# Hash-bucket attention before a relu-squared layer: attention in double steps of two key blocks, a shared ring of score banks, totals ahead of the last values

## The chip, the core and the metric

The kernel runs on one core of a Trainium2 chip. Engines with queues of their own work side by side: TensorE (PE, matmuls, with its weight loads, PEld, beside them), VectorE (DVE), ScalarE (ACT), GpSimd (POOL) and SyncE (SP, which here only issues DMAs). They meet in semaphores. Matmul results land in PSUM, which this kernel divides into 8 banks of 128 partitions x 512 float32. The metric is the device time of one execution in microseconds (us); the time of a kernel is the median of its runs.

## The reference

Attention in which a query sees only keys of its own hash bucket (six sign bits of a projection), and then a layer with squared relu. The bridge between the two lays the heads side by side.

```python
B, H, S, D = 4, 8, 768, 64
q_bits = (np.einsum('bhsd,dk->bhsk', q, proj) > 0)          # k_bits likewise
mask = q_bucket[:, :, :, None] == k_bucket[:, :, None, :]
scores = np.where(mask, scale * np.matmul(q, k.transpose(0, 1, 3, 2)), -1e9)
attn = np.exp(scores - scores.max(-1)); attn = attn / (attn.sum(-1) + 1e-09)
x = np.matmul(attn, v)                                      # -> (3072, 512)
r = np.maximum(x @ w_in, 0.0)                               # w_in 512 x 2048, float64 input
return (r * r) @ w_out                                      # w_out 2048 x 512, float64 input
```

## The kernel before

**Attention** goes over 16 pairs of heads (`pr`), each with six key blocks of 128 (`kt`). For a block, `score` computes the scores of all 768 queries against 128 keys for both heads of the pair: two cuts of the queries (512 and 256), each with two bf16 matmuls of hash bits, which push unequal buckets far down, and two float32 matmuls of features. Each cut has a PSUM tile of two banks, one bank a head (`st0`, `st1`, one buffer each), and ACT writes the exponential into `e`, a ring of four. `attend` multiplies `e` into the values, which accumulate in `xo` (two banks) over the six blocks. `add_up` keeps the running sum of the `e` tiles on DVE (`total`).

The end of a pair: `sum_up` adds over keys by matmuls with ones (`tot`), DVE transposes (`flip`), forms the reciprocal (`once`) and places it (`both`); `spread` carries it to the right partitions with one matmul into the last columns of `tot`'s bank, and DVE transposes that to `recs`; `normalize` multiplies `xo` by it into `x_t`, which SP stores to `x_all`.

The next pair is prepared meanwhile: `features` transposes q and k on DVE, `hash_bits` projects them on PE, `signs` makes bits of them on ACT, `weigh` scales the key bits on DVE. Two rotating banks (`bank`) serve `tot` and the hash.

The program order is that of the code; there is no scheduler. One step `u` is one key block: the score of block u, the spread if a pair ended, the hash of the next pair where the table `PREPARE` has it (block 3), the values of block u - 2, `sum_up` behind the values of block 4, and so on. Every engine takes its part of this order.

The **weights** come as float64 and are rounded to float32 in 32 pieces by integer operations on DVE (`part_weight`, `round_weight`) and ACT (`place_power`); the table `w_steps` spreads them over attention, two pieces a pair. `sums_in` and `sums_x` form sums of w_in and of x on DVE for the next stage, in the steps at the start of six pairs.

The **token stage** runs over three chunks of 1024 tokens. Both products are done by a scheme with seven products in place of eight, the second by it twice over (49 `leaf` tiles of w_out). In a chunk, `hidden(i, r)` for r = 0 to 7 multiplies x with `w_unit` r (SP loads it from the stored sums of w_in, two steps ahead): 28 matmuls of 512 columns, five results that ACT copies (`one`, `two`, `five`, `three`, `h`), and relu-squared on DVE. `project(i)` then multiplies with the leaves. During chunk 0, four sets of rows of w_out (`load_rows`) are turned into leaves: `sums_out(m)` forms first the smaller sums (`factors`), then `sums` in a single buffer, and POOL stores both to `w_out_49` in seven DMAs. That happens behind r = 0, 1, 3, 5 (`WHEN`). When the fourth is formed, its memory is given up for the buffers of the leaves, of which the first five are asked for at r = 6, on ACT's queue; such a transfer waits until the stores that read the old memory are done.

Lines that the prediction uses: L389 the score matmuls, L417 attend, L328 the hash, L435 the totals, L459 the spread, L394 the exponential, L644 all matmuls of the token stage, L651 ACT's copies there, L486 to L489 the sums, L545 `w_unit`, L773 the leaves.

Of the kernel before, what the change touches and what calls it, by code (L numbers as in the profile page):

```python
# [8 lines left out]
FP32 = mybir.dt.float32  # L9
# [25 lines left out]
def kernel(  # L35
# [257 lines left out]
    def first_features(w, r):  # L293

        if r == 0:
            feat[0, w] = p_f.tile([P, S], FP32, name=f"feat{w}")
        tp = bank("tp")
        for i in range(SB // 2):
            t = r * (SB // 2) + i
            nc.tensor.transpose(  # L300
                out=tp[:, i * P:(i + 1) * P],
                in_=nat[0, ("q_nat", "k_nat")[w]][:, t].rearrange("p h d -> p (h d)"),
                identity=ident,
            )
        out = feat[0, w][:, r * HS:(r + 1) * HS]
        if w == 0:
            nc.scalar.copy(out=out, in_=tp[:, 0:HS])
        else:
            nc.vector.tensor_copy(out=out, in_=tp[:, 0:HS])
# [8 lines left out]
    def hash_bits(pr, ws=(0, 1), banks=None):  # L318


        banks = banks or (bank("hash0"), bank("hash1"))
        for w in ws:
            hashed[pr, w] = banks
            for c in range(2):
                g = 2 * w + c
                for h in range(2):
                    rows = slice(h * D, (h + 1) * D)
                    nc.tensor.matmul(  # L328
                        out=banks[h][g * NR_B:(g + 1) * NR_B, 0:HS], lhsT=projs[rows],
# [3 lines left out]
    def signs(pr, w):  # L333
        bits[pr, w] = t = all_bits[pr % 2][w]
        for c in range(2):
            at = slice((2 * w + c) * NR_B, (2 * w + c + 1) * NR_B)
            for h in range(2):
                nc.scalar.activation(  # L338
                    out=t[h * D:h * D + NR_B, c * HS:(c + 1) * HS], in_=hashed[pr, w][h][at, 0:HS],
                    func=ACTF.Sign, scale=HUGE, bias=lifts[at],  # L340
                )

    def first_keys():

        bits[0, 1] = t = all_bits[0][1]
        for c in range(2):
            at = slice((2 + c) * NR_B, (3 + c) * NR_B)
            cut = slice(c * HS, (c + 1) * HS)
            for h in range(2):
                nc.vector.tensor_scalar(  # L350
                    out=t[h * D:h * D + NR_B, cut], in0=hashed[0, 1][h][at, 0:HS],
# [7 lines left out]
    def weigh(pr):  # L359
# [4 lines left out]

    PREPARE = (
        (),
        ((features, 0),),
        ((features, 1),),
        ((hash_bits,), (signs, 1)),
        ((signs, 0), (weigh,)),  # L370
        (),
    )

    weights = {}

    def score_banks(c):
        return ps_s.tile([P, 2, 512], FP32, name=f"st{c}")

    def score(pr, kt):
# [4 lines left out]
        sts = [score_banks(c) for c in range(2)]  # L384
        for st, (lo, hi) in zip(sts, CUTS):
# [7 lines left out]
        for st, (lo, hi) in zip(sts, CUTS):  # L393
# [780 lines left out]
```

## Time and profile before

| | us |
|---|---|
| runs shown | 936.61, 937.38, 939.73; median 937.38 |
| the profiled execution, device time | 935.12 |
| its span, first to last instruction | 933.4 |
| before the first score of pair 1 | 32.20 |
| pairs 1 to 14 | 307.88 |
| pair 15 and the end of attention | 26.49 |
| token stage | 566.83 |

| engine | busy us of 933.4 |
|---|---|
| PE | 902.5 |
| PEld | 492.8 |
| DVE | 697.8 |
| ACT | 363.4 |
| POOL | 91.4 |

The busy shares say that PE is the engine to look at. The mean clock granted to it was 0.995. PE's idle time has few places: the start, the end of attention, and some waits in chunk 0 of the token stage. In the timeline a row joins consecutive instructions of one kind: start, duration from the first start to the last end, operation, names, shape, count, and in brackets the idle time ahead of it with what ended it. A float32 matmul counts as two instructions there. Matmuls overlap at their ends, so the cost of one kind is read from the start of one row to the start of the next.

### The profile page before, as it was taken

Reading aid. Unit: us, or ns where it says so; the run is one execution under the profiler, and the core shown is the slowest. Engines: PE = TensorE matmul, PEld = TensorE weight load, DVE = VectorE, ACT = ScalarE, POOL = GpSimd, SP = SyncE. Lnnn points to the kernel's source line nnn. Section 1 sums busy time; section 2 is a strip of 40 time slices with the busy share of each in tenths; the row PEclk is TensorE's granted clock in tenths of the full one; section 3 lists DMA queues with packets and bytes.
Section 4 is the critical chain, followed back from the end, with each engine's and each line's share of the span. In section 5 each row is a group of like instructions: output and inputs, shape, how many; then the busy total and the mean of one; then the engine's idle time right before and its main releaser. Section 6 shows DMA issues by size and latency. Waiting matters only on the chain.

```text
span 933.4 us, 11806 instructions
## 1 busy us (share of the span) xinstructions
PE 902.5 (97%) x4326; PEld 492.8 (53%) x4326; DVE 697.8 (75%) x1010; ACT 363.4 (39%) x593; POOL 91.4 (10%) x149
## 2 busy tenths in 40 slices
PE   6999999999999999989799999999999999999995
PEld 2334343343334433434378884444888744448884
DVE  4777887788877776867876785667977856679775
ACT  4877777777767773212111112222111122221110
POOL 2000000000000000442300020111100211110002
PEclk9999999999999999999999999999999999999998
DMA  9665975799975422997885574556856634455565
GB/s 184 132 113 113 253 174 116 158 275 248 225 142 135 116 79 86 263 297 203 255 279 154 163 149 96 146 147 198 293 156 166 136 113 138 137 154 157 152 168 104
DMA packets 253343, 158.14 MB, mean 169 GB/s; under 512 B 166432, under 2 KB 215584, under 8 KB 253280
## 3 DMA queue, kind: packets, MB, share of 16 engines
q1 hardware_dynamic: 219264, 83.12, 38.6%
q10 hardware_dynamic: 23280, 38.81, 14.1%
q0 software_dynamic: 10736, 35.40, 12.5%
q8 instruction: 36, 0.59, 0.3%
q14 instruction: 27, 0.22, 0.1%
HBM read 119.28 MB, written 38.01 MB: 169 GB/s over the span
## 4 chain that ended last, share of the span: by engine, by line
PE 86%; DMA 6%; DVE 4%; issue 1%; ACT 1%; POOL 1%; SPq 0%; DVEq 0%; ACTq 0%
PE acc L644 50%; PE st L389 17%; PE xo L417 14%; DMA w_unit<-w_in 3%; PE tot L435 2%; PE hash L328 2%; DMA leaf<-w_out 1%; DMA w_out<-sums 1%; DMA out_dram<-ot 1%; PE tot L459 1%; DVE b L734 1%; POOL w_out L933 1%; ACT e L394 0%; DMA k_nat<-in_k_dram 0%; DVE h L733 0%
## 5 line engine op out<-in xcount | busy, mean ns | idle before, releaser
L394 ACT ACTIVATE e<-st 128x1024 f32<-128x1024 f32 x192 | 145.3, 810 | 87.4 <-PE st L389 87.0
L644 PE MATMUL acc<-x,w_unit 128*128 128x512 f32 x384 | 169.5, 593 | 0.6 <-DMA w_unit<-w_in 0.6
L389 PE MATMUL st<-feat,feat 64*128 64x512 f32 (+1 forms) x768 | 150.3, 483 | 0.0
L417 PE MATMUL xo<-e,v_nat 128*64 128x512 f32 (+1 forms) x768 | 144.9, 498 | 0.2 <-DVE x_t L472 0.2
L644 PE MATMUL acc<-t_x,w_unit 128*128 128x512 f32 x288 | 129.6, 600 | 7.2 <-ACT one L651 7.1
L644 PE MATMUL acc<-b,leaf 128*128 128x256 f32 x600 | 133.2, 379 | 0.2 <-DMA leaf<-w_out 0.2
L644 PEld LDWEIGHTS acc<-b,leaf 128*128 128x128 f32 x600 | 113.9, 190 | 17.4 <-issue 1.4
L644 PEld LDWEIGHTS acc<-x,w_unit 128*128 128x128 f32 x384 | 72.8, 190 | 91.5 <-issue 89.0
L644 PEld LDWEIGHTS acc<-t_x,w_unit 128*128 128x128 f32 x288 | 54.9, 192 | 78.6 <-issue 68.2
L417 PEld LDWEIGHTS xo<-e,v_nat 128*64 128x64 f32 x768 | 46.9, 136 | 86.5 <-issue 84.4
L407 DVE TENSOR_TENSOR total<-total,e 128x1536 f32<-128x1536 f32 x48 | 83.5, 1740 | 1.1 <-ACT e L394 1.0
L389 PEld LDWEIGHTS st<-feat,feat 64*128 64x128 f32 x768 | 66.5, 189 | 33.9 <-issue 31.5
L733 DVE TENSOR_TENSOR h<-acc,two 128x512 f32<-128x512 f32 x24 | 16.6, 691 | 86.6 <-PE acc L644 86.6
L644 PE MATMUL acc<-t,leaf 128*128 128x256 f32 x336 | 76.5, 380 | 0.3 <-DVE t L492 0.3
L651 ACT COPY two<-acc 128x512 f32<-128x512 f32 (+1 forms) x45 | 21.9, 486 | 132.7 <-PE acc L644 129.6
L338 ACT ACTIVATE bits<-hash,lifts 32x384 bf16<-32x384 f32 x120 | 68.6, 572 | 4.8 <-PE hash L328 3.3
L644 PEld LDWEIGHTS acc<-t,leaf 128*128 128x128 f32 x336 | 63.7, 190 | 9.7 <-DVE t L492 1.1
L651 ACT COPY one<-acc 128x512 f32<-128x512 f32 (+1 forms) x45 | 21.9, 486 | 120.1 <-PE acc L644 65.1
L389 PE MATMUL st<-bits,bits 64*128 64x256 bf16 (+1 forms) x384 | 63.6, 328 | 4.3 <-ACT e L394 2.5
L734 DVE SCALAR_TENSOR_TENSOR b<-h 128x512 f32<-128x512 f32 x96 | 64.3, 690 | 2.9 <-DMA x_all<-x_t 0.5
L644 PE MATMUL acc<-b_t,leaf 128*128 128x256 f32 x240 | 54.2, 380 | 1.3 <-issue 1.3
L389 PEld LDWEIGHTS <-bits 64*128 64x128 bf16 x384 | 18.9, 93 | 68.3 <-issue 67.9
(125 smaller groups left out, 898.8 us busy)
## 6 DMA issues: line engine op xcount, KB each, us to landing
leaf<-w_out ACTq DMA_DIRECT2D x147, 256.0 KB, 3.0
w_unit<-w_in SPq DMA_DIRECT2D x24, 896.0 KB, 5.4
raw<-in_moe_w_in_dram SPq DMA_DIRECT2D x16, 512.0 KB, 4.3
raw<-in_moe_w_out_dram SPq DMA_DIRECT2D x16, 512.0 KB, 3.9
w_out<-sums POOLq DMA_DIRECT2D x16, 448.0 KB, 8.2
v_nat<-in_v_dram SPq DMA_DIRECT2D x16, 384.0 KB, 4.3
x_all<-x_t SPq DMA_DIRECT2D x16, 384.0 KB, 3.0
x<-x_all POOLq DMA_DIRECT2D x3, 2048.0 KB, 12.0
```

What stands on the lines that cost most here:

```text
L328: nc.tensor.matmul(out=banks[h][g * NR_B:(g + 1) * NR_B, 0:HS], lhsT=projs[rows], rhs=feat[pr, w][rows, c * HS:(c + 1) * HS], start=True, ...
L338: nc.scalar.activation(out=t[h * D:h * D + NR_B, c * HS:(c + 1) * HS], in_=hashed[pr, w][h][at, 0:HS], func=ACTF.Sign, scale=HUGE, bias=li ...
L389: nc.tensor.matmul(out=st[:, h, 0:hi - lo], lhsT=src[pr, 1][rows, key], rhs=src[pr, 0][rows, lo:hi], start=first, stop=not first,)
L394: nc.scalar.activation(out=e[:, :, lo:hi], in_=st[:, :, 0:hi - lo], func=ACTF.Exp, scale=scale)
L407: nc.vector.tensor_tensor(out=totals[pr], in0=in0, in1=weights[pr, kt][:, :, 0:S], op=ALU.add)
L417: nc.tensor.matmul(out=xo[h * D:(h + 1) * D, lo:hi], lhsT=nat[pr, "v_nat"][:, h, kt * D:(kt + 1) * D], rhs=weights[pr, kt][:, h, lo:hi], s ...
L435: nc.tensor.matmul(out=tot[g * 32:(g + 1) * 32, 0:HS], lhsT=ones, rhs=src[:, h, c * HS:(c + 1) * HS], start=src is totals[pr], stop=src is ...
L459: nc.tensor.matmul(out=rec, lhsT=picks, rhs=both.rearrange("p c n -> p (c n)"), start=True, stop=True)
L644: nc.tensor.matmul(out=acc[to], lhsT=a(i), rhs=b(i), start=first and i == 0, stop=last and i == n - 1, skip_group_check=True,)
L651: nc.scalar.copy(out=t, in_=acc[of])
L733: nc.vector.tensor_tensor(out=h, in0=one, in1=two, op=ALU.add)
L734: nc.vector.scalar_tensor_tensor(out=out[:, r], in0=h, scalar=0.0, in1=h, op0=ALU.max, op1=ALU.mult)
```

## The change

Attention goes in double steps: two scores, then the values of two blocks. In pair `pr` the order on PE is: scores 0 and 1; `finish` of the pair before (the hash of the pair after, the totals, the values of blocks 4 and 5, the spread); scores 2 and 3; values 0 and 1; scores 4 and 5; values 2 and 3. The totals so stand ahead of the last two values. One pool of three double banks, taken in turn, serves the score tiles, the totals, the hash and the first transposes. The spread's result goes to the last 24 columns of `xo`, by two matmuls of 64 output partitions instead of one of 128, and the transpose to `recs` moves into `normalize`. Both feature tiles of the next pair are made ahead of a pair's first score, and the weight pieces, loads and sums are put at fixed places of a pair; sums follow at a pair's end.

At the start, all transposes come ahead of both hashes, and pair 1 is loaded before the first values. In the token stage the second set of `sums` is formed and stored behind r = 2 instead of 1 (`THEN`), its `factors` still behind r = 1; `load_unit` stands ahead of the leaves; and the first five leaves of chunk 0 are asked for on SP's queue.

```diff
-    ps_s = first.enter_context(tc.tile_pool(name="ps_s", bufs=1, space=PSUM))
+    ps_s = first.enter_context(tc.tile_pool(name="ps_s", bufs=3, space=PSUM))
-    ps_1 = first.enter_context(tc.tile_pool(name="ps_1", bufs=2, space=PSUM))
-    def bank(name):
-        return ps_1.tile([P, 512], FP32, name=name, tag="bank")
+    def turn(name):
+        return ps_s.tile([P, 2, 512], FP32, name=name, tag="turn")
...
     def spread(pr):
-        both, tot = onces.pop(pr)
-        rec = tot[:, HS:HS + 2 * NB]
-        nc.tensor.matmul(
-            out=rec, lhsT=picks, rhs=both.rearrange("p c n -> p (c n)"), start=True, stop=True
-        )
...
+        both = onces.pop(pr)
+        rec = outs[pr][:, 1024 - 2 * NB:]
+        for h in range(2):
+            nc.tensor.matmul(
+                out=rec[h * D:(h + 1) * D], lhsT=picks[:, h * D:(h + 1) * D],
+                rhs=both.rearrange("p c n -> p (c n)"), start=True, stop=True,
+            )
+        recs[pr] = rec
...
+    def finish(pr, beside=None):
+        tot = turn("tot")
+        if beside:
+            beside()
+        sum_up(pr, tot)
+        for kt in (SB - 2, SB - 1):
+            attend(pr, kt)
+        spread(pr)
...
+        first_features(0)
+        first_features(1)
         for w in range(2):
+            hash_bits(0, turn("hash"), (w,))
         signs(0, 0)
         first_keys()
+        for pr in range(NP):
+            a, b = 2 * pr, 2 * pr + 1
+            more = pr + 1 < NP
+            def prepare():
+                hash_bits(pr + 1, turn("hash"))
+                for w in (1, 0):
+                    signs(pr + 1, w)
...
+            if more and pr > 0:
+                for w in range(2):
+                    features(pr + 1, w)
+            if pr > 0:
+                round_weight(b - 2)
+                load_weight(b)
+            score(pr, 0)
+            score(pr, 1)
+            if pr > 0:
+                finish(pr - 1, prepare if more else None)
+            add_up(pr, 1)
...
+            if pr > 0:
+                normalize(pr - 1)
...
+            part_weight(a)
+            score(pr, 2)
+            score(pr, 3)
+            if pr == 0:
+                prepare()
+            place_power(a)
+            attend(pr, 0)
+            attend(pr, 1)
+            for kt in (2, 3):
+                add_up(pr, kt)
...
+            round_weight(a)
+            part_weight(b)
...
+            score(pr, 4)
+            score(pr, 5)
+            place_power(b)
+            attend(pr, 2)
+            attend(pr, 3)
+            add_up(pr, 4)
+            if pr in sums:
+                f, n = sums[pr]
+                f(n)
+        finish(NP - 1)
+        normalize(NP - 1)
+        round_weight(2 * NP - 1)
...
-        def load_leaf(n):
+        def load_leaf(n, early=False):
...
-                nc.scalar.dma_start(out=leaves[k, m], in_=w_out_49[OUTER[k][0], :, m])
+                queue = nc.sync if early else nc.scalar
+                queue.dma_start(out=leaves[k, m], in_=w_out_49[OUTER[k][0], :, m])
...
-        NOUT, WHEN = 2, (0, 1, 3, 5)
+        NOUT, WHEN, THEN = 2, (0, 1, 3, 5), (0, 2, 3, 5)
...
                 if i == 0 and r in WHEN:
-                    m = WHEN.index(r)
-                    sums_out(m)
+                    sums_out(WHEN.index(r))
+                if i == 0 and r in THEN:
+                    m = THEN.index(r)
+                    sums_out_49(m)
...
+                load_unit(i * NR + r + (3 if i == 0 and r < 2 else 2))
                 if r == NR - 2:
                     for n in range(NLEAF - 2):
-                        load_leaf(n)
-                load_unit(i * NR + r + (3 if i == 0 and r < 2 else 2))
+                        load_leaf(n, i == 0)
```

The first place is PE at the end of a pair. Before, the totals came behind the values of block 4 (`e_119`), with those of block 5 (`e_120`) still to come; these are the rows around `tot` in a middle pair.

```order
L417 MATMUL xo<-e_119,v_nat 64x512 x2
L417 MATMUL xo<-e_119,v_nat 64x257 x2
L435 MATMUL tot<-total,ones 32x384 x4
L435 MATMUL tot<-e_120,ones 32x384 x4
L389 LDWEIGHTS bits_0_122
```

In the changed program the same place reads so, again in a middle pair; the row ahead is the last of score 1.

```order
L375 MATMUL st<-feat_2105,feat_2107 128x256 x2
L327 MATMUL hash<-feat_2298,projs 32x384 x4
L327 MATMUL hash<-feat_2300,projs 32x384 x4
L420 MATMUL tot<-total,ones 32x384 x4
L420 MATMUL tot<-e_115,ones 32x384 x4
L402 MATMUL xo<-e_114,v_nat 64x512 x2
L402 MATMUL xo<-e_114,v_nat 64x257 x2
L402 MATMUL xo<-e_115,v_nat 64x512 x2
L402 MATMUL xo<-e_115,v_nat 64x257 x2
L445 MATMUL xo<-both,picks 64x24 x2
```

The hash moved here from behind score 3, and the totals, both last values and the spread now stand in one run, behind two scores of the next pair.

The second place is DVE behind `hidden(0, 1)` of the token stage, where the second set of factors and sums is formed. Before:

```order
L492 TENSOR_TENSOR b_t<-b_3246,b_3245 128x512
L486 TENSOR_TENSOR factors<-other,factors 128x512
L487 TENSOR_TENSOR factors<-factors,other 128x512
L488 TENSOR_TENSOR factors<-factors 128x512
L489 TENSOR_TENSOR factors<-factors 128x512
L486 TENSOR_TENSOR sums<-factors 128x896
L487 TENSOR_TENSOR sums<-factors 128x896
L488 TENSOR_TENSOR sums<-sums,factors 128x896
L489 TENSOR_TENSOR sums<-factors,sums 128x896
L492 TENSOR_TENSOR b_3246<-b_3248,b_3246 128x512
L733 TENSOR_TENSOR h<-acc_3396,one 128x512
```

And now:

```order
L481 TENSOR_TENSOR b_t<-b_3241,b_3240 128x512
L475 TENSOR_TENSOR factors<-other,factors 128x512
L476 TENSOR_TENSOR factors<-factors,other 128x512
L477 TENSOR_TENSOR factors<-factors 128x512
L478 TENSOR_TENSOR factors<-factors 128x512
L481 TENSOR_TENSOR b_3241<-b_3243,b_3241 128x512
L746 TENSOR_TENSOR h<-acc_3373,one 128x512
```

The four operations on `sums` left this place; they follow the next r-step.

The third place is the queue that asks for the first leaves. Before, it was ACT, between the copies of r = 6 and those of r = 7:

```order
L651 COPY three<-acc_3598 128x512
L731 COPY h<-acc_3598 128x512
L773 DMA leaf<-w_out_66 128x512 x5
L651 COPY one<-acc_3652 128x512
L651 COPY two<-acc_3652 128x512
```

Now it is SP, behind the units up to that of the next chunk's first step:

```order
L519 DMA w_unit<-w_in_63 128x14x128 x6
L787 DMA leaf<-w_out_66 128x512 x5
L519 DMA w_unit<-w_in_63 128x14x128
L818 DMA out_dram<-ot 32x16x32 x24
```

Nothing stands now between ACT's copies of r = 6 and r = 7, and the five leaves have one w_unit and then the output stores behind them on SP.

More of the change, by code (lines that the diff above doesn't have):

```diff
@@ L316, with hash_bits @@
     hashed = {}
-    def hash_bits(pr, ws=(0, 1), banks=None):
-        banks = banks or (bank("hash0"), bank("hash1"))
+    def hash_bits(pr, banks, ws=(0, 1)):
         for w in ws:
@@ L328, in hash_bits @@
                     nc.tensor.matmul(
-                        out=banks[h][g * NR_B:(g + 1) * NR_B, 0:HS], lhsT=projs[rows],
+                        out=banks[g * NR_B:(g + 1) * NR_B, h, 0:HS], lhsT=projs[rows],
                         rhs=feat[pr, w][rows, c * HS:(c + 1) * HS], start=True, stop=True,
@@ L425, with sum_up @@
     onces = {}
-    def sum_up(pr):
-        tot = bank("tot")
+    def sum_up(pr, tot):
+        tot = tot[:, 0]
         for src in (totals[pr], weights[pr, SB - 1]):
```

156 lines of the change are left out of this document (53 added, 103 removed).

## The prediction

> **What bounds the kernel now.** I read the stages first, since a share of the whole span mixes attention with the product that follows it. The rows below are busy time by stretch of time; after the stretch and its length come TensorE (PE), its weight loads, VectorE (DVE), ScalarE (ACT), GpSimd, the granted clock, the DMA share and GB/s. The cuts are the first score of the second head pair (32.20), that of the last pair (340.08) and the first matmul of the token stage (366.57).
>
> ```profile
> 32.20:340.08 307.88, 307.61 (x2156) 122.08 (x2157) 255.16 (x347) 228.55 (x339) 0.79 (x1) 1.00 0.73 171
> 340.08:366.57 26.49, 25.09 (x174) 10.23 (x173) 16.79 (x25) 12.04 (x17) 0.00 (x0) 1.00 0.11 41
> 366.57:933.40 566.83, 547.00 (x1852) 350.81 (x1851) 409.06 (x591) 103.63 (x210) 84.59 (x126) 0.99 0.63 176
> ```
>
> In the fourteen middle pairs PE is busy for 307.61 of 307.88 us, so nothing but less time on PE makes them shorter: 307.88 / 14 = **21.99 us a pair**. The last pair and the token stage hold idle time, 1.4 and 19.8 us.
>
> What PE spends a pair on is in its timeline (start, duration, operation). Durations overlap, since matmuls are pipelined, so I use start to start.
>
> ```profile
> 170.93 0.40 PE L459 MATMUL tot<-both,picks 128*128 128x24 f32 x2
> 171.26 1.51 PE L417 MATMUL xo<-e,v_nat 128*64 128x512 f32 x8
> 172.71 0.39 PE L389 MATMUL st<-bits,bits 64*128 64x512 bf16 x2
> 172.94 1.02 PE L389 MATMUL st<-feat,feat 64*128 64x512 f32 x4
> 173.80 0.27 PE L389 MATMUL st<-bits,bits 64*128 64x256 bf16 x2
> 173.91 0.60 PE L389 MATMUL st<-feat,feat 64*128 64x256 f32 x4
> 174.43 1.51 PE L417 MATMUL xo<-e,v_nat 128*64 128x512 f32 x8
> ...
> 177.60 1.23 PE L328 MATMUL hash<-feat,projs 64*32 64x384 f32 x16
> 178.77 1.51 PE L417 MATMUL xo<-e,v_nat 128*64 128x512 f32 x8
> ...
> 189.71 0.85 PE L435 MATMUL tot<-total,ones 128*32 128x384 f32 x8
> 190.38 0.83 PE L435 MATMUL tot<-e,ones 128*32 128x384 f32 x8
> 191.14 0.39 PE L389 MATMUL st<-bits,bits 64*128 64x512 bf16 x2
> ```
>
> A score (S) takes 174.43 - 172.71 = 1.72, an attend (A, weights times values) 172.71 - 171.26 = 1.45, the hash 1.17, the totals 1.43, the spread 0.33. Six S, six A and the three others make 19.02 + 2.93 = 21.95, which is the period. The same run shows what it costs to go from one kind to the other. The 512-column half of S takes 173.80 - 172.71 = 1.09; the 256-column half should take half of that, 0.545, and takes 0.63, so leaving S for A costs about 0.09 and S alone is 1.635. For A there is one place with three in a row:
>
> ```profile
> 359.40 4.10 PE L417 MATMUL xo<-e,v_nat 128*64 128x512 f32 x24
> 363.44 0.85 PE L435 MATMUL tot<-total,ones 128*32 128x384 f32 x8
> 364.11 0.83 PE L435 MATMUL tot<-e,ones 128*32 128x384 f32 x8
> 366.33 0.40 PE L459 MATMUL tot<-both,picks 128*128 128x24 f32 x2 [1.40 <-DVE both L449]
> ```
>
> Three take 4.04, so one more costs (4.04 - 1.45) / 2 = 1.30, and entering and leaving A cost 0.15. A visit to A between scores costs 0.15 + 0.09 = **0.24**.
>
> **The change, part by part.**
>
> *Double steps.* S and A now alternate two by two: three visits a pair instead of six. The new pair: three S S (2 x 1.635 + 0.09 = 3.36 each, 10.08); two A A between scores (2 x 1.30 + 0.15 = 2.75, 5.50); one A A behind the totals (2.65); totals 1.43; hash and spread below. Saved in S and A: 3 x 0.24 = 0.72.
>
> *Hash.* It took 1.17 because its second half waited for a transposed feature tile on DVE. In the first pair, where both tiles are there, it takes 23.00 - 22.19 = 0.81:
>
> ```profile
> 12.57 0.39 PE L389 MATMUL st<-bits,bits 64*128 64x512 bf16 x2 [1.81 <-DVE bits L354]
> ...
> 14.94 0.39 PE L389 MATMUL st<-bits,bits 64*128 64x512 bf16 x2 [0.57 <-ACT e L394]
> ...
> 22.19 0.88 PE L328 MATMUL hash<-feat,projs 64*32 64x384 f32 x16
> 23.00 1.51 PE L417 MATMUL xo<-e,v_nat 128*64 128x512 f32 x8
> ```
>
> The new program has DVE make both tiles ahead of the pair's first score, so I take 0.81, bounded by 0.81 and 1.17.
>
> *Spread.* Two matmuls of half the width stand behind A A, with A's shape, into A's own bank. No row shows this form. Bounds: 0.13 (the 24 columns added as a share of A's time per column, with one start) is below what the row of one 24-column matmul with both switches took, 0.33, and two of those would be 0.66. I take 0.25, nearest the one measured.
>
> Sum of a pair: 10.08 + 5.50 + 2.65 + 1.43 + 0.81 + 0.25 = **20.72**; 14 x (21.99 - 20.72) = **-17.8**.
>
> *Does anything stall in its place?* Three places decide. First, the ring of three score banks. The exponential of the 512-column half starts 1.30 after its S and takes 1.03 (S at 191.14 above):
>
> ```profile
> 192.44 1.03 ACT L394 ACTIVATE e<-st 128x1024 f32<-128x1024 f32 x1 [1.67 <-PE st L389]
> ```
>
> A double step takes four banks; the fourth is the first again, free 1.30 + 1.03 = 2.33 after the start, and wanted at 1.635 + 1.09 = 2.73: 0.4 to spare. The totals reuse the third bank, whose exponential starts no earlier than 1.635 + 1.30 = 2.94 and ends at 3.97; the totals are wanted at 3.36 + 0.81 = 4.17: 0.2 to spare. Were the cover gone, each late exponential would hold PE for what it is late, and behind it stand the last values and the spread. Second, the reciprocal: spread came 366.33 - 363.44 = 2.89 after the totals with DVE free, a row above; A A now lies between and takes 2.65 of it plus the 1.43 of the totals themselves, so it is covered. Third, DVE, whose work is the same but regrouped: in the pair with the most of it, where a quarter of the input sums is formed, it is busy 19.52 of 21.93 us.
>
> ```profile
> 169.21:191.14 21.93, 21.93 (x158) 8.71 (x155) 19.52 (x27) 16.25 (x24) 0.00 (x0) 1.00 0.67 181
> ```
>
> In a pair of 20.72 that leaves 1.2, less the places where DVE waits for ACT or PE; covered, but barely, in six pairs. ACT has 16.25 of work.
>
> *Start.* The first score waits 1.81 for the key bits. All transposes now come ahead of both hashes, and the first keys' features are copied without a hash between. I expect -1.2 there, and -0.2 from the first pair's fewer visits net of its own waits for exponentials (0.57 each now): **-1.4**, bounds 0 and -3 (all of 1.81, two times 0.57).
>
> *Last pair.* The 26.49 of the second row become one pair without hash (19.91) plus totals, A A and spread (1.43 + 2.65 + 0.25): 24.24, **-2.3**; the 1.40 wait for the reciprocal goes, since A A stands in it.
>
> *Token stage.* The second set of factor sums is formed and stored one r-step later, and the first five leaves of w_out go out on SP's queue, behind the w_unit of that step, instead of ACT's.
>
> ```profile
> PE acc L644 <- ACT one L651: 7.1, 2, 4.8
> ...
> PE acc L644 <- DMA w_unit<-w_in: 0.6, 1, 0.6
> ```
>
> ```profile
> 400.94 1.09 DVE L486 TENSOR_TENSOR sums<-factors 128x896 f32<-128x896 f32 x1 [4.65 <-DMA w_out<-sums]
> ```
>
> The waits of PE for one ACT copy are 2.3 and 4.8 us. The first stems from DVE, which stood 4.65 for the earlier sums to be stored; with the second sums an r-step later their buffer is free. The third set then follows after one r-step, 28 matmuls or some 12 us, with its own smaller sums ahead of it, where before the second followed in less because DVE was late with the first; I expect no wait there. The second stems from ACT's own queue:
>
> ```profile
> 455.83 6.05 ACTq L773 DMA_DIRECT2D leaf<-w_out  x5
> 461.98 0.58 ACT L651 COPY one<-acc 128x512 f32<-128x512 f32 x1 [5.97 <-DMA w_out<-sums]
> ```
>
> Five leaf transfers hold ACT for 6.05 us until those stores land, with the copy behind them. On SP's queue they hold only SP, and behind them there is just the next w_unit. After this gap PE ran at a granted clock of 0.53 for 3.6 us, which costs 3.6 x 0.47 = 1.7 more:
>
> ```profile
> 462.40:466.00 3.60, 3.38 (x4) 1.50 (x5) 1.38 (x2) 0.16 (x1) 0.00 (x0) 0.53 1.02 365
> ```
>
> The Trainium skill, "TensorE: Matmul & The Clock Gate", section "Why this matters for your kernels", warns of PE-idle gaps above about 3 us, after which the clock falls back; the trace agrees with 4.8 us and 0.53. By that rule a wait for leaves of 2.6 us would leave the clock alone and the sum as it stands, and one of 5 would bring the 1.7 back.
>
> So 2.3 + 0.6 + 4.8 + 1.7 = 9.4 can go. What is late next are the leaves, behind 0.9 MB of w_unit in the same queue.
>
> ```profile
> w_unit<-w_in SPq DMA_DIRECT2D x2, 896.0 KB, 16.4
> ```
>
> ```profile
> leaf<-w_out ACTq DMA_DIRECT2D x5, 256.0 KB, 8.9
> ```
>
> ```profile
> 472.93 1.24 PE L644 MATMUL acc<-b,leaf 128*128 128x256 f32 x5
> ```
>
> The leaf products would start at 472.93 - 9.4 = 463.5 (on the old clock of events). If leaves land as before, 8.9 after an issue at 455.83 - 2.9, they are there (461.8): no wait. If they follow w_unit, issued near 451.5 and landed 16.4 later, the first arrives at about 468: 4.5. I take 2.6, between them: **-6.8**, bounds 0 and -9.4.
>
> **Sum**: -17.8 - 1.4 - 2.3 - 6.8 = -28.3. The profiled execution (935.12 us, its span 933.4) would be at 906.8; the median of the runs lies 2.3 above it, 937.38, so I give **909.1** against that.
>
> **Rivals.**
>
> 1. *The token stage's waits only move* (24%). For it: 0.9 MB of w_unit takes 16.4 us beside the stores, and moved stores may meet another w_unit; against it: waits of an engine off the path have slack here, 19.8 us idle in 567. It gives attention's 21.5 alone: 937.4 - 21.5 = **915.9**.
> 2. *DVE becomes the bound in the full pairs* (12%). For it: 19.52 of a 20.72 pair, and the next pair's features stand behind the sums; a hash that waits for them holds totals and values behind it. At 1.5 us in six pairs it gives back 9: **918**. Against it: the other pairs show DVE idle, 255.16 of 307.88 busy.
> 3. *The change of kind costs nothing by itself* (8%): 0.24 would be a shadow of the shapes, so that double steps save only the hash, the spread, start and waits, 0.72 x 15 = 10.8 less: **920**. Against it: the three A in a row take 4.04 and not 4.35.
> 4. *Slower: scores back to back run into the exponential* (5%). At the start, where each S must wait for the last one's banks, S comes every 14.94 - 12.57 = 2.37 with 0.57 idle: 0.73 more than 1.635. If the second score of every double step paid that, 48 x 0.73 = 35 would be lost against 28.3 gained: **944**. It decides once PE waits above 28.3 / 48 = 0.59 per double step. Against it: the third bank, by which the fourth half is 0.4 late-proof; a margin of 0.2 at the totals is the weakest.
>
> **How the numbers follow.** My forecast, 909 within 4 us, has 51%. The range takes in rival 1 and most of 2 and reaches down to all 9.4 in the token stage and a cheap start: **902 to 918.5**, with rivals 3, 4 and their like outside. A difference of 0.3%, 2.8 us, is about what a measurement of this kernel can tell from no change. Forecast and rivals 1 to 3 are all faster by far more: faster 0.94, same 0.02 (several stalls at once), slower 0.04.
>
> **What would show it.** Right: in the middle pairs PE still has no idle time and first scores lie 20.7 apart; spread starts without a wait; PE's two waits for the ACT copy are gone and the clock stays at 1.00 there; the leaf products wait under 3 us. Wrong: waits of scores or totals for the exponential, of the hash for features in pairs with sums, of w_unit or leaf above 3 us, or a second A that takes 1.45.

## The result, and the profile after

The changed kernel takes **909.25 us** (median of 4 runs, 908.39 to 909.83) against 937.25 of the kernel before (4 runs, 936.61 to 939.73): ratio 0.970, 95% interval 0.968 to 0.972. The forecast was 909.1. That is closer than its parts were, as the stages show. They are cut at the same events as before: first score of pair 1, first score of pair 15, first matmul of the token stage. Columns are as in the prediction (length, busy time of PE, PEld, DVE, ACT, POOL, clock, DMA share, GB/s); this is the changed kernel.

```profile
35.17:322.92 287.75, 287.75 (x2188) 131.41 (x2187) 253.31 (x343) 227.77 (x336) 0.79 (x1) 1.00 0.76 176
322.92:346.90 23.98, 23.98 (x178) 10.97 (x176) 15.94 (x24) 11.56 (x16) 0.00 (x0) 1.00 0.18 61
346.90:906.50 559.60, 545.64 (x1854) 350.12 (x1850) 410.65 (x594) 104.01 (x210) 84.80 (x126) 1.00 0.64 179
0.00:35.17 35.17, 25.17 (x149) 11.85 (x150) 17.55 (x51) 20.81 (x31) 6.09 (x22) 1.00 1.04 171
```

| stage | before, us | after, us | change | forecast |
|---|---|---|---|---|
| to the first score of pair 1 | 32.20 | 35.17 | +3.0 | -1.4 |
| 14 middle pairs | 307.88 | 287.75 | -20.1 | -17.8 |
| last pair | 26.49 | 23.98 | -2.5 | -2.3 |
| token stage | 566.83 | 559.60 | -7.2 | -6.8 |
| span | 933.4 | 906.5 | -26.9 | -28.3 |

PE is busy in all 287.75 us of the middle pairs: no stall took the place of what was removed, and a pair takes 20.55. The start went the wrong way by 4.4 us against its forecast, and the pairs gave 2.3 more than theirs. That 28.3 forecast and 26.9 measured both end near 909 is also due to which run was profiled: that of the changed kernel, 908.39, lies 0.9 below its median, that of the kernel before, 935.12, lay 2.3 below the one it was held against.

PE in a middle pair of the changed kernel (start, duration, operation), from the hash to the second double step:

```profile
38.51 0.88 PE L327 MATMUL hash<-feat,projs 64*32 64x384 f32 x16
39.31 0.85 PE L420 MATMUL tot<-total,ones 128*32 128x384 f32 x8
39.98 0.83 PE L420 MATMUL tot<-e,ones 128*32 128x384 f32 x8
40.74 2.81 PE L402 MATMUL xo<-e,v_nat 128*64 128x512 f32 x16
43.38 0.26 PE L445 MATMUL xo<-both,picks 128*64 128x24 f32 x4
43.56 0.39 PE L375 MATMUL st<-bits,bits 64*128 64x512 bf16 x2
...
46.90 2.81 PE L402 MATMUL xo<-e,v_nat 128*64 128x512 f32 x16
49.64 0.39 PE L375 MATMUL st<-bits,bits 64*128 64x512 bf16 x2
```

From start to start: hash 0.80, totals 1.43, A A behind them 2.64, spread 0.18, S S 46.90 - 43.56 = 3.34, A A 2.74. Each is the term of the forecast (0.81, 1.43, 2.65, 0.25, 3.36, 2.75) or a little less, and no row has a wait in brackets.

What PE waits for in the token stage of the changed kernel is short now (total, times, longest, from the waits of PE):

```profile
PE acc L657 <- DMA leaf<-w_out: 2.3, 2, 2.1
...
PE acc L657 <- DMA w_unit<-w_in: 0.6, 1, 0.6
PE acc L657 <- ACT one L664: 0.5, 2, 0.3
```

The waits for ACT's copy of 2.3 and 4.8 are gone, and the leaves are late by 2.1, where the forecast had 2.6. The 0.6 for a w_unit stayed.

### The profile page after: what moved, and what is told of

Its sections match the earlier page's. It is cut to its first block, busy times and chain, and to the rows that moved or that the text cites. A ratio compares the mean times of both kernels' runs of the same rounds, so it can differ in the third digit from the quotient of the medians.

```text
span 906.5 us, 11859 instructions
## 1 busy us (share of the span) xinstructions
PE 882.5 (97%) x4358; PEld 504.4 (56%) x4358; DVE 697.4 (77%) x1010; ACT 364.2 (40%) x593; POOL 91.7 (10%) x149
## 4 chain that ended last, share of the span: by engine, by line
PE 90%; DMA 4%; DVE 2%; ACT 1%; issue 1%; POOL 0%; ACTq 0%; SPq 0%; DVEq 0%
PE acc L657 54%; PE st L375 18%; PE xo L402 14%; DMA w_unit<-w_in 3%; PE tot L420 3%; PE hash L327 1%; ACT bits L337 1%; DMA out_dram<-ot 1%; DVE peaks L698 0%; DMA q_nat<-in_q_dram 0%; PE tp L300 0%; POOL out_dram L818 0%; DVE b L747 0%; ACTq L787 0%; DVE ot L811 0%
## 5 line engine op out<-in xcount | busy, mean ns | idle before, releaser
L375 PE MATMUL st<-feat,feat 64*128 64x512 f32 (+1 forms) x768 | 152.4, 488 | 0.0
L402 PE MATMUL xo<-e,v_nat 128*64 128x512 f32 (+1 forms) x768 | 134.8, 492 | 0.0
L402 PEld LDWEIGHTS xo<-e,v_nat 128*64 128x64 f32 x768 | 51.4, 136 | 82.4 <-issue 70.9
L337 ACT ACTIVATE bits<-hash,lifts 32x384 bf16<-32x384 f32 x124 | 71.1, 573 | 6.5 <-PE hash L327 3.2
L657 PEld LDWEIGHTS acc<-b_t,leaf 128*128 128x128 f32 x240 | 45.4, 190 | 8.1 <-issue 2.1
```

The costliest lines, as they stand in the source:

```text
L337: nc.scalar.activation(out=t[h * D:h * D + NR_B, c * HS:(c + 1) * HS], in_=hashed[pr, w][at, h, 0:HS], func=ACTF.Sign, scale=HUGE, bias=li ...
L375: nc.tensor.matmul(out=st[:, h, 0:hi - lo], lhsT=src[pr, 1][rows, key], rhs=src[pr, 0][rows, lo:hi], start=first, stop=not first,)
L402: nc.tensor.matmul(out=xo[h * D:(h + 1) * D, lo:hi], lhsT=nat[pr, "v_nat"][:, h, kt * D:(kt + 1) * D], rhs=weights[pr, kt][:, h, lo:hi], s ...
L657: nc.tensor.matmul(out=acc[to], lhsT=a(i), rhs=b(i), start=first and i == 0, stop=last and i == n - 1, skip_group_check=True,)
```

## The experiments

Each kernel is the changed one with the edit shown, unless the table names another to start from. Times are medians; "span" is that of its profiled run, to be held against 906.5. Stages are cut as above.

| run | us | range | edit |
|---|---|---|---|
| changed kernel | 909.25 | 908.39 to 909.83 | |
| single_steps | 930.49 | 929.32 to 932.87 | blocks 2 to 5 in single steps |
| single_end | 912.23 | 910.29 to 912.79 | blocks 4 and 5 in single steps |
| ring_of_two | 1020.24 | 1019.49 to 1022.00 | two double banks for scores |
| totals_behind | 944.09 | 943.12 to 945.73 | totals behind the last values |
| leaves_on_act | 912.29 | 911.57 to 914.12 | first leaves on ACT's queue |
| sums_early | 914.33 | 913.91 to 917.11 | second sums behind r = 1 |
| start_mixed | 908.27 | 905.85 to 912.42 | start in halves, query hash early |
| mixed_warm | 908.95 | 906.86 to 912.00 | start_mixed, idle matmuls first |
| triple_steps | 915.07 | 914.62 to 915.48 | steps of three |
| triple_deferred | 902.82 | 901.27 to 903.13 | start_mixed, steps of three, ACT's work moved |
| triple_warm | 902.25 | 899.61 to 903.82 | triple_deferred, idle matmuls first |
| leaves_ahead | 901.69 | 900.02 to 903.34 | triple_deferred, leaves ahead of w_unit |

### What a visit to the values costs: single_steps and single_end

```diff
             score(pr, 2)
-            score(pr, 3)
+            attend(pr, 0)
+            score(pr, 3)
...
-            attend(pr, 0)
             attend(pr, 1)
...
             score(pr, 4)
+            attend(pr, 2)
             score(pr, 5)
...
-            attend(pr, 2)
             attend(pr, 3)
```

> The changed kernel, but with blocks 2 to 5 in single steps again: score 2, values 0, score 3, values 1, score 4, values 2, score 5, values 3 (in the first pair score 3 stays beside score 2). Nothing else moves. Theory (a visit to the values between scores costs PE 0.24 us): 31 more visits x 0.24 = 7.4 us, so 909.3 + 7.4 = 916.7. Rival (a change of kind costs nothing by itself): 909.3, within 1 us.

Measured: 930.5, 21 us more, almost three times what was expected. The waits of PE in single_steps say that an unplanned one came with it:

```profile
PE xo L402 <- PE st L375: 12.5, 15, 0.9
```

```profile
176.63 1.51 PE L402 MATMUL xo<-e,v_nat 128*64 128x512 f32 x8 [0.85 <-PE st L375]
```

```profile
175.51 1.02 DVE L461 SCALAR_TENSOR_TENSOR x_t<-xo,recs 128x768 f32<-128x768 f32 x1
```

Fifteen times the values of block 0 stood 0.8 us. The profile names PE itself as what ended that wait, which can't be. The values now come a score earlier, and x_t of the pair before still reads `xo` on DVE: it ends at 176.53, and the values begin 0.1 later. This run doesn't tell the visit from the wait, so the second one moves only blocks 4 and 5, where no x_t is in reach.

> The changed kernel, but only blocks 4 and 5 of each pair in single steps: score 4, values 2, score 5, values 3. The values of block 0 stay where they were, so that the wait for x_t that the run single_steps showed cannot come. Theory (a visit costs PE 0.24 to 0.26 us): 16 more visits, 3.8 to 4.2 us, 913.0 to 913.5, with no new wait of PE. Rival (the added time of single_steps was its waits, the visits are free): 909.3, within 1 us.

Measured: 912.23, and the middle pairs of single_end:

```profile
33.57:324.99 291.42, 291.42 (x2186) 127.71 (x2185) 255.85 (x343) 227.54 (x337) 0.79 (x1) 1.00 0.75 175
```

PE is busy throughout, as in the changed kernel, and the 14 pairs take 291.42 - 287.75 = 3.67 more for one visit each: **0.26 us a visit** with nothing waited for. The theory holds, and the rival that the change of kind is free falls. (The median came 0.8 to 1.3 below what was expected. In the profiled run pair 1 begins 1.6 earlier, at 33.57: in the first pair a wait of 1.2 for an exponential at score 5 is down to 0.2. The token stage, which the edit leaves alone, takes 1.7 more.) The rest of single_steps fits: its pairs take 1.55 more, of which 0.52 are visits and 0.83 the wait; 0.2 I can't place.

### What the ring of three is for: ring_of_two

```diff
-    ps_s = first.enter_context(tc.tile_pool(name="ps_s", bufs=3, space=PSUM))
+    ps_s = first.enter_context(tc.tile_pool(name="ps_s", bufs=2, space=PSUM))
...
-        tot = turn("tot")
-        if beside:
-            beside()
-        sum_up(pr, tot)
+        sum_up(pr, apart("tot"))
         for kt in (SB - 2, SB - 1):
             attend(pr, kt)
+        if beside:
+            beside()
```

> The changed kernel, but with two double banks in turn for the scores and the third for the totals and the hash alone; so that the bank is free, the hash goes behind the last values. Theory (the third double bank keeps the second score of a double step from the exponential): the second score's first bank is free 2.36 us after the first score's start instead of being wanted at 1.635, 0.73 x 48 = 35 us, so 944. Rival (the ring's depth does not matter, ACT has time): 909 to 911.

Measured: 1020, over twice the expected loss. PE waits 77 us in ring_of_two, in 48 places; the rows show two kinds.

```profile
PE st L380 <- ACT e L384: 77.1, 48, 3.9
```

```profile
191.50 0.61 PE L380 MATMUL st<-bits,bits 64*128 64x512 bf16 x2 [3.93 <-ACT e L384]
...
197.29 0.39 PE L380 MATMUL st<-bits,bits 64*128 64x512 bf16 x2
...
199.66 0.39 PE L380 MATMUL st<-bits,bits 64*128 64x512 bf16 x2 [0.58 <-ACT e L384]
```

```profile
185.72 4.67 ACT L342 ACTIVATE bits<-hash,lifts 32x384 bf16<-32x384 f32 x8 [4.07 <-PE hash L332]
190.42 1.51 ACT L384 ACTIVATE e<-st 128x1024 f32<-128x1024 f32 x2
```

Where nothing else is on ACT the second score comes 199.66 - 197.29 = 2.37 after the first, 0.74 later than its 1.63: the mechanism and size of the slower rival, in 2 of 3 double steps. In the third ACT does the eight hash signs first, 4.67 us, and with two double banks PE has to stand for nearly all of that. That part comes from where I put the hash for this run as much as from the ring, and after 3.9 us of idleness PE is slow as well (the first row's 0.61 for 0.39). In its 14 middle pairs PE is not only idle for 71 us but also busy 34.5 us longer than in the changed kernel's, at a mean clock of 0.93. So the run shows that the ring carries the double steps, and 0.74 is the price of a second score without it; it gives no clean total.

### What lies between totals and spread: totals_behind

```diff
-        sum_up(pr, tot)
         for kt in (SB - 2, SB - 1):
             attend(pr, kt)
+        sum_up(pr, tot)
         spread(pr)
```

> The changed kernel, but with the totals behind the values of blocks 4 and 5 instead of ahead. Theory (the last values cover the reciprocal): spread comes 2.89 us after the totals' start, of which 1.43 are the totals themselves, so PE waits 1.46 in each of 16 pairs, 23 us: 932.6. Rival (spread waits anyway for little, DVE being ahead): 909 to 912.

Measured: 944.1, 35 more, and 11.5 above what was expected. PE's waits in totals_behind:

```profile
PE xo L445 <- DVE both L434: 22.4, 16, 1.5
...
PE xo L402 <- DVE x_t L461: 4.3, 14, 0.3
```

The wait for the reciprocal is what was expected, 22.4 of 23. A second one follows from it: spread later, `recs` and x_t later, and the next pair's first values stand 0.3 in 14 pairs. I had not followed the chain that far. The 14 middle pairs take 318.67 us, 30.9 more than in the changed kernel, which is 2.2 a pair: 23.9 are idle time of PE, and in the other 7.1 PE is busy for longer, which I didn't take apart. The last pair takes 3.1 more and the token stage 1.7. With the totals behind, the change would have been slower than the kernel before.

### The token stage: leaves_on_act and sums_early

```diff
-                        load_leaf(n, i == 0)
+                        load_leaf(n)
```

> The changed kernel, but the first five leaves asked for on ACT's queue again; all else stays. Theory (on ACT's queue they hold ACT's copies, and PE behind them, until the stores land): PE's wait of 4.8 and 1.7 of lower clock come back, the wait of the leaf products (2.3) goes: +4.2, 913.5. Rival (the wait only moved from ACT's copy to the leaf, its length set by the stores): 909.3, within 1 us.

Measured: 912.3, 3.0 more. In leaves_on_act the middle pairs are the same to 0.01 us, and the token stage of the profiled run takes 564.38, 4.8 more; the profiled run of the changed kernel lay 0.9 below its median, which is part of the difference between 4.8 and 3.0. Its waits and the stretch behind the longest:

```profile
PE acc L657 <- ACT one L664: 4.9, 3, 4.2
```

```profile
440.10:443.50 3.40, 3.40 (x6) 1.34 (x5) 0.37 (x1) 0.59 (x1) 0.00 (x0) 0.50 1.05 370
```

The wait for the copy is back (4.2), the wait for the leaves is gone, and the clock is at 0.50 for 3.4 us: 4.2 - 2.3 + 1.7 = 3.6 of the 4.8; the rest I can't place. The rival, a wait that only moves, falls: the queue is what mattered.

```diff
-        NOUT, WHEN, THEN = 2, (0, 1, 3, 5), (0, 2, 3, 5)
+        NOUT, WHEN, THEN = 2, (0, 1, 3, 5), (0, 1, 3, 5)
```

> The changed kernel, but the second set of sums formed and stored behind r = 1 again; all else stays. Theory (DVE stands for the single buffer of sums, ACT's h copy and PE behind it): PE's wait of 2.3 comes back, 911.5. Rival (with attention changed, the wait is hidden or another store takes its place): 909.3, within 1 us.

Measured: 914.3, 5.1 more, and in the profiled run 8.5 in the token stage. PE's waits in sums_early:

```profile
PE acc L657 <- DMA leaf<-w_out: 3.1, 1, 3.1
PE acc L657 <- ACT one L664: 2.4, 2, 2.2
...
PE acc L657 <- DMA w_unit<-w_in: 1.9, 1, 1.9
```

```profile
401.20:404.60 3.40, 3.40 (x5) 1.35 (x4) 3.33 (x5) 0.58 (x1) 0.98 (x1) 0.50 0.44 105
452.40:455.80 3.40, 2.86 (x7) 2.32 (x8) 1.52 (x4) 0.00 (x0) 0.00 (x0) 0.50 1.08 376
```

The expected 2.2 for the copy is there. Beside it the w_unit is 1.3 later and the leaves 0.8 later than in the changed kernel, and two stretches of 3.4 us run at half the clock, 1.7 each. The profiled run took 917.11 and the other four between 913.91 and 914.43, so whether these had both stretches at half clock is not known. By the medians, undoing one edit costs 3.0 or 5.1, 8.1 together, and the kernel before, with both undone, had a token stage longer by 7.2: these numbers don't show whether the two simply add.

### The start: start_mixed and mixed_warm

The start of the changed kernel on PE, up to the first of the third score:

```profile
4.82 0.87 PE L300 MATMUL tp<-ident,q_nat 128*128 128x128 f32 x3 [4.82 <-DMA q_nat<-in_q_dram]
6.26 0.90 PE L300 MATMUL tp<-ident,q_nat 128*128 128x128 f32 x3 [0.57 <-ACT feat L307]
6.96 0.85 PE L300 MATMUL tp<-ident,k_nat 128*128 128x128 f32 x3
8.45 0.90 PE L300 MATMUL tp<-ident,k_nat 128*128 128x128 f32 x3 [0.65 <-DVE feat L309]
9.29 2.21 PE L327 MATMUL hash<-feat,projs 64*32 64x384 f32 x16
13.26 0.63 PE L375 MATMUL st<-bits,bits 64*128 64x512 bf16 x2 [1.76 <-ACT bits L337]
13.64 1.96 PE L375 MATMUL st<-feat,feat 64*128 64x512 f32 x4
...
16.42 0.68 PE L375 MATMUL st<-bits,bits 64*128 64x512 bf16 x2
...
18.82 0.40 PE L375 MATMUL st<-bits,bits 64*128 64x512 bf16 x2
```

Two things stand out. Both halves of a transpose share a tile, and the second half waits for the copy of the first (0.57, 0.65). And the float32 matmuls of the first score's longer half take 1.96 instead of 1.02: PE runs at half its pace, though the profile grants a clock of 1.00 there. The first two scores take 18.82 - 13.26 = 5.56 instead of 2 x 1.63, 2.3 too long. With the first score 0.7 later than in the kernel before (13.26 for 12.57) that makes the 3.0.

```diff
-        tp = turn("tp")
-        for r in range(2):
+        for r in rs:
+            tp = turn("tp")
...
         first_features(0)
-        first_features(1)
-        for w in range(2):
-            hash_bits(0, turn("hash"), (w,))
+        first_features(1, (0,))
+        hash_bits(0, turn("hash"), (0,))
+        first_features(1, (1,))
+        hash_bits(0, turn("hash"), (1,))
```

> The changed kernel, but at the start each half of the transposes has its own turn of banks, and the query hash comes ahead of the second half of the key transposes, as in the kernel before. The loads keep their new order. Theory (the start lost its time since halves in one tile wait for each other's copies, the query bits come 2 us later, and PE is slow until it has worked without a gap for some 4 us): first score near 12.6 instead of 13.3 and at full pace, 2.5 us less, 906.7. Rival (what holds the first pair is the new order of loads, or the waits inside the pair): 909, within 0.7.

Measured: 908.3, with a range that takes in 909.25, so the time alone says little; the profile says more. PE in start_mixed:

```profile
13.15 0.39 PE L376 MATMUL st<-bits,bits 64*128 64x512 bf16 x2 [1.76 <-issue]
13.36 1.04 PE L376 MATMUL st<-feat,feat 64*128 64x512 f32 x4
```

```profile
32.70:320.45 287.75, 287.75 (x2186) 131.40 (x2186) 253.29 (x343) 227.56 (x336) 0.79 (x1) 1.00 0.76 177
```

The first score comes only 0.1 earlier, not 0.7, but it runs at full pace, and pair 1 begins at 32.70 instead of 35.17: 2.5 less, as expected, with middle pairs equal to 0.01. So the order of transposes and hashes, with the loads left alone, can give that part back. It doesn't secure it. leaves_ahead, a later run whose start has the same order as start_mixed, came to its first score at half pace all the same, and its third score begins at 19.59, where start_mixed has 16.38 and the changed kernel 18.82. PE in leaves_ahead (the first row is busy time from 6.49 to 11.78):

```profile
6.49:11.78 5.29, 5.28 (x22) 1.55 (x22) 1.12 (x2) 2.35 (x5) 0.51 (x6) 1.00 1.51 153
```

```profile
9.57 2.21 PE L328 MATMUL hash<-feat,projs 64*32 64x384 f32 x8
13.54 0.61 PE L376 MATMUL st<-bits,bits 64*128 64x512 bf16 x2 [1.76 <-issue]
13.92 1.93 PE L376 MATMUL st<-feat,feat 64*128 64x512 f32 x4
```

Of the profiled runs, all eight with the changed kernel's order begin at half pace, and of three with the order of start_mixed and no warm-up (start_mixed, triple_deferred, leaves_ahead) one does. What decides it there is open. The start of the kernel before still was 0.5 shorter: inside the first pair PE waits for the hash's bank (0.6) and, at score 5, for signs and exponentials (0.4 and 1.2).

To see whether PE's pace sets the start, mixed_warm has PE work from the beginning, while the first loads are under way:

```diff
+        idle = turn("idle")
+        for i in range(NWARM):
+            nc.tensor.matmul(
+                out=idle[0:32, 0, 0:P], lhsT=warm[:, 0:32], rhs=warm, start=True, stop=True
+            )
```

> start_mixed, and ahead of the first transposes, while the first loads are under way, 14 matmuls on a tile of zeros whose result nobody reads. Theory (PE runs at half its pace until it has worked some 4 us without a gap, and so the first transposes and hashes take twice their time): transposes of 0.15 us each instead of 0.29, first score 1.5 to 2.4 us earlier than in start_mixed (13.15), all after it moved alike, 906 against its 908.3. Rival (the start goes by the arrival of q and k, and by ACT's and DVE's bits, at their own pace): first score moved by less than 0.7, 908.

Measured: 908.95. PE in mixed_warm:

```profile
1.08 5.57 PE L560 MATMUL idle<-warm 128*32 128x128 f32 x28 [1.08 <-DVE excess L228]
6.58 0.87 PE L301 MATMUL tp<-ident,q_nat 128*128 128x128 f32 x6
...
13.21 0.39 PE L376 MATMUL st<-bits,bits 64*128 64x512 bf16 x2 [1.76 <-issue]
```

The six transposes take 0.87 instead of 1.51, so the pace is there, but the first score stays at 13.2, as the rival had it; the expectation's 1.5 to 2.4 was wrong. Why it stays this run doesn't show cleanly. The idle matmuls last until 6.65, so that the transposes of q begin at 6.58 instead of 4.83, and what PE gains in pace it may have lost there. That ACT's and DVE's bits set the moment is argued, not shown.

### Further along the same way: triple_steps, triple_deferred, triple_warm, leaves_ahead

If visits are what counts, steps of three blocks save one more.

```diff
-    NRING = 4
+    NRING = 6
...
-            score(pr, 0)
-            score(pr, 1)
+            for kt in range(3):
+                score(pr, kt)
...
-        for kt in (SB - 2, SB - 1):
+        for kt in (SB - 3, SB - 2, SB - 1):
             attend(pr, kt)
```

> The changed kernel with steps of three: scores 0, 1, 2; totals, hash, values 3, 4, 5 and spread of the pair before; scores 3, 4, 5; values 0, 1, 2. The ring of exponentials has six tiles instead of four. Theory (visits are what counts, and three double banks carry three scores because ACT needs 1.5 us for what PE does in 1.63): one visit less in 15 pairs, 3.6 to 4 us less, 905.5. Rival (the third score runs into the exponential, or DVE's sums come too late): a wait of PE in every pair and 910 to 920.

Measured: 915.1, slower than the changed kernel. PE waits for an exponential in 15 places (8.6 us), and ACT in triple_steps shows why its exponentials are late:

```profile
182.01 0.72 ACT L158 ACTIVATE small<-power,excess 128x512 uint8<-128x512 uint32 x1 [2.42 <-DVE power L141]
182.76 0.63 ACT L159 ACTIVATE power<-small 128x512 uint32<-128x512 uint8 x1
183.30 4.41 ACT L379 ACTIVATE e<-st 128x1024 f32<-128x1024 f32 x6
```

ACT stands for DVE with a weight piece, and the exponentials follow at 183.30, although PE began the first of their scores at 181.12 and the exponential elsewhere starts 1.3 behind that. In the next run that piece follows the exponentials of the next pair.

```diff
+            if pr > 0:
+                place_power(b - 2)
+                finish(pr - 1, prepare if more else None)
```

> start_mixed with steps of three as in triple_steps, but ACT's part of the second weight piece comes after the first three exponentials of the next pair instead of ahead of them, and the first pair keeps its double steps for blocks 0 to 3. Theory (triple_steps lost since that ACT work, waiting for DVE, stood ahead of the exponentials): no wait of PE for the exponential in the middle pairs, 20.3 us a pair, 3.4 to 3.6 less than start_mixed: 904.8. Rival (three scores in a row overrun three double banks whatever stands beside them): again waits of about 0.4 to 0.6 a pair, 909 or more.

Measured: **902.8**, ratio to the kernel before 0.964 (0.962 to 0.966), below the changed kernel's interval. Its middle pairs:

```profile
29.86:316.16 286.30, 284.93 (x2186) 135.46 (x2185) 255.54 (x345) 228.68 (x338) 0.79 (x1) 1.00 0.73 177
```

They take 286.30, 20.45 each, with 1.4 us of waits for feature tiles; a pair without waits takes 20.30 in the timeline, 0.25 less than with two blocks, which is one visit. The rival of triple_steps had the waits and the time right, but the scores' own exponentials were not the cause: with ACT's weight piece behind them, three scores in a row run through without a wait in the middle pairs. (The edit also moves DVE's part of that piece, `round_weight`, behind `normalize`; the two moves are not told apart.) The step from the changed kernel is larger than the visit, though. Between the profiled runs of start_mixed and triple_deferred lie 4.5 us, and the middle pairs give only 1.45 of them; the token stage, whose program is the same, gives 1.25, and the first and last pair 1.8, of which 1.2 is the wait for an exponential that the new order of the first pair no longer has. Two variants of it: triple_warm adds the idle matmuls of mixed_warm,

> triple_deferred together with the 14 matmuls of mixed_warm ahead of the first transposes (on the tile that later serves as flip, since memory is full). Theory: the gains add, being at different places: 902.5. Rival (a steady pair with less slack gives the start's gain back): no better than triple_deferred.

and leaves_ahead changes the order of leaves and w_unit on SP's queue.

```diff
-                load_unit(i * NR + r + (3 if i == 0 and r < 2 else 2))
                 if r == NR - 2:
                     for n in range(NLEAF - 2):
                         load_leaf(n, i == 0)
+                load_unit(i * NR + r + (3 if i == 0 and r < 2 else 2))
```

> triple_deferred, but with the first five leaves asked for ahead of the w_unit of the next chunk's first step on SP's queue, the order that the kernel before had between the two; in triple_deferred, as in the changed kernel, they stand behind it. Theory (the leaf products wait 2.2 us because the leaves land only behind 0.9 MB of w_unit in the same queue): that wait falls below 0.5, 2 us less than triple_deferred, 900.8. Rival (the leaves' landing is set by the stores that they wait for, wherever they stand): the wait stays above 1.5, 902.8.

Measured: 902.25 and 901.69, and both ranges overlap that of triple_deferred, so neither edit is shown to gain. In leaves_ahead the wait of 2.2 for leaves at the start of the leaf products is gone, as its theory said, and a wait of 1.3 for ACT's copy and 0.3 for a later leaf came; its token stage takes 558.06 against 558.31. Taken away on its own, that wait only moved.

## Why the prediction was right, and where it was not

*What bounds the pairs, and double steps.* Right, by its own mechanism: PE was busy throughout, before and after. A visit was put at 0.24 and measured at 0.26. Pairs were forecast at 20.72 and took 20.55; of the 0.17, 0.07 is the spread, for which I took 0.25 between 0.13 and 0.66 and which takes 0.18, 0.06 the three double scores (3.34 for 3.36) and the rest the other terms. One term of the sum, the 2.65 for A A behind the totals, stood there without its working; it measured 2.64.

*Nothing stalls in its place.* Right in the middle pairs. The margins that decided were real: without the third double bank, 0.74 per second score; with the totals behind, a wait of 1.4 a pair for the reciprocal and 2.2 a pair in all.

*Start.* This step failed: "All transposes now come ahead of both hashes ... I expect -1.2 there". I counted the hash that no longer stood between the copies and not what now stood ahead of the query bits. The transposes wait for copies by the shared tile, the signs of the query start at 10.9 instead of 8.9, the first score comes 0.7 later, and PE comes to it at half pace, which costs 2.3 in the first two. The size changes from run to run: in three runs with the same start (leaves_on_act, totals_behind, sums_early) pair 1 begins at 34.47, 34.78 and 35.34. The bounds, 0 and -3, did not hold +3.0 either; they allowed for less waiting but not for a new wait or a slow PE.

The Trainium skill, "TensorE: Matmul & The Clock Gate", section "Why this matters for your kernels", asks for 4 us of continuous work to reach full pace. Two starts agree: 4.6 us without a gap in start_mixed (6.76 to 11.38) and full pace at 13.15; 3.05 in the changed kernel (8.45 to 11.50) and half pace. A third does not: 5.3 us without a gap in leaves_ahead (6.49 to 11.78) and still half pace at 13.92. So 4 us were not always enough here.

*Last pair.* Right: -2.5 for -2.3; spread no longer waits.

*Token stage.* Right in sum (-7.2 for -6.8) and in its queue argument. The 2.6 for the leaves was a middle between 0 and 4.5, so that 2.05 came near it is partly luck; that w_unit ahead of them makes them late is borne out by leaves_ahead, where the order is turned and that wait is gone. Wrong in one term: the 0.6 for a w_unit, which the forecast let go without a reason, did not go. The 1.7 of lower clock did: the leaf wait of 2.05 left it at 1.00 in the profiled run; the other three runs were 0.6 to 1.4 us longer at a mean clock of 0.994 against 0.998. That mean counts the idle end too, where the profile shows 0.50 (from 902.7 to 906.5 in the changed kernel), so what lowered it there is open.

*Rivals.* None came about as the whole: the token stage's waits got shorter and did not only move, DVE did not bind any of the six full pairs, the change of kind is not free, and scores did not run into the exponential in any middle pair. That the last can happen is shown by ring_of_two.

So the median was met to 0.2 us partly by luck: 4.4 too good at the start, 2.9 too little elsewhere, and a profiled run that lay nearer to its median after than before.

## What to carry to other kernels

On an engine that never waits, look at the order of kinds: the row with three in a run against one alone gave 0.24 a visit from the profile of before, single_end measured 0.26, and with enough banks for the longer runs three visits a pair could be taken out and then a fourth. Before a start-up is reordered, write down for each result that the first real work needs when its inputs come and who shares its tile: here copies on ACT and DVE (0.57 and 0.65) and the bits (1.76) held PE, none of which the order on PE alone shows. And after each move follow the engine beside it: in steps of three it was ACT's weight piece, which had nothing to do with scores, that decided the sign.

## What was not expected of the hardware

The length of one gap does not tell whether the clock falls. In sums_early the stretch at 0.50 from 401.2 follows a gap of PE of only 1.93 us (ended at 399.85) some 11 us after one of 2.25, whereas the 2.05 of the changed kernel and the 2.73 of single_end left the clock at 1.00. What set the drop off is not shown, but the forecast's reckoning that a wait of 2.6 us would leave the clock alone was not safe. And at the start PE worked at half pace (1.96 for 1.02) while the granted clock read 1.00; there the durations, not the clock column, tell the pace. With the same order of work that pace came and went: start_mixed and triple_deferred reached the first score at full pace, leaves_ahead at half.
